# A decode step's forward and backward pass on one Trainium2 core: two zero fills at other places, and one late weight load through another queue

## The chip, the core and the metric

The kernel runs on one core of a Trainium2 chip. The core has a matrix engine (TensorE, PE in the profile), a vector engine (VectorE, DVE), an activation engine (ScalarE, ACT), GpSimd (POOL) and SyncE (SP), and 16 DMA engines that move data between the chip's memory (DRAM) and the core's on-chip memory. Two engines issue nearly all the transfers here: GpSimd, whose transfers stand in the profile as queue q0 (software_dynamic), and SyncE, queue q1 (hardware_dynamic). The metric is the device time of one execution in microseconds, as the median of several runs. Lower is better.

## What is computed

The reference is one token's pass through a transformer block with conditioning, and the gradients of all its inputs:

```python
mod = (silu(c) @ w_mod).reshape(c.shape[0], 6, 1, -1)   # sa, ca, ga, sb, cb, gb
h = layernorm(x) * (1 + ca) + sa
x = x + ga * attention(h, k_cache, v_cache, wq, wo)     # last 4096 of 65536 positions
h = layernorm(x) * (1 + cb) + sb
x = x + gb * glu(h, w_gate, w_up, w_down)               # sigmoid(h@w_gate) * (h@w_up) @ w_down
out, vjp = jax.vjp(f, x, k_cache, v_cache, wq, wo, w_gate, w_up, w_down, c, w_mod)
```

There are 11 outputs: the block's output and ten gradients. Two of them, the gradients of the two caches, have the caches' full size (4 heads by 65536 positions by 128), but attention reads the last 4096 positions only. So the first 61440 positions of each head are zeros, and the kernel has to write these zeros. They are 120 pieces of 1 MB, by far the largest part of what the kernel writes. The rest is the gradient of every weight matrix.

## The kernel before

**Stages.** The kernel first loads the first third of `w_mod`, the cache window, `A_wq` and the value window. It computes the modulation, the query and the scores of all 32 heads (the K pass), and the softmax. In the N passes (the loop over `g` and `t_`, 4 groups by 32 tiles, 128 steps; matmuls in line 737 into `n_ps`) it forms a matrix for each head from keys, values and probabilities. A long chain of matmuls with `A_wo` follows (`bch`, line 796, `b_ps`). Then come the feed-forward blocks `q` = 0 to 6 (`front`, `turn`), which load `w_up`, `w_gate` and `w_down` block by block, and last the weight gradients: outer products that DVE computes into a buffer of the arena, each sent to DRAM by one store of about 1 MB.

**The order is written out by hand.** The kernel is scheduled manually: each engine executes its instructions in the order of the source. GpSimd's queue in particular holds loads, zero fills and gradient stores in one fixed order, and an instruction that waits holds up everything behind it on that engine. Each issuing engine's DMAs also wait for the semaphore that they use; GpSimd's DMAs take eight semaphores in turn.

**Zero fills.** `zero(n, after)` takes the next `n` pieces from the list `zleft` and issues one DMA for each on GpSimd. If `after` is given, GpSimd waits for that instruction first. There are three kinds. A plain fill writes 1 MB from the tile `zeros` (line 209). In the N passes and in `bch`, pieces whose region is one row are copied from a piece of DRAM that is already zero (`big`, line 203). Six pieces, at fixed places in the list, are narrow: a tiny DMA (line 194) and 960 KB (line 197). How many pieces are taken at which place stands in constants at the top: `Z_SM` behind the softmax (line 595), `Z_N` over the 128 steps of the N passes (line 740; `spread(total, n)` deals `total` evenly over `n`), `Z_FFN` in the blocks, and `Z_HAND` behind the stores of the gradient of `w_down` near the end of the blocks.

**Stores of the gradient of `w_down`.** `dwd(q, off, outer)` computes four outer products into the 8 KB per partition at `off` and returns the store (line 1138). In block 5 stands `dwd(0)` with `zero(Z_HAND[0])` behind it, and at the end of the block `dwd(1)` with `zero(Z_HAND[1])`, `turn(6)`, and `dwd(2, 152)` with `zero(Z_HAND[2])`. Block 6 has `dwd(3)` with `zero(Z_HAND[3])`, and `dwd(4)` with `zero(Z_HAND[4])` follows. `dwd(5, 152)`, inside `layernorm_bwd_col`, uses the same place of the arena as `dwd(2, 152)`. The feed-forward's own loads of `w_down` go out on SyncE.

**The last stage.** `dw_rows(k, j, off)` writes one 128-row piece of the gradient of `w_up` or `w_gate` (store in line 1130), `sec(j)` one piece of the gradient of `w_mod`: it reduces the last sixth of `w_mod` against a row into `dcs` (the instruction of line 253), forms an outer product over the same buffer (line 249) and stores it (line 1260). For `j` < 6 that sixth is already on the chip. For `j` = 6 and 7 `sec_load(j)` fetches it, 256 KB each, into a part of `sec_t[j]`. `dwq_tile` (line 1308), `s2` (line 1312) and `kv_store` (line 1304) store the other gradients.

The order around `sec_load` in the source is: `dw_rows(1, 6)`, `dw_rows(1, 7)`, `sec(2)`, `sec(3)`, `sec_load(6)`, `sec_load(7)`, then the scores' gradient, and `grad_kv`, within which `sec(4)`, `dwq_tile(0)`, `sec(5)`, `dwq_tile(1)`, `sec(6)`, `dwq_tile(2)` stand at steps 8, 16 and 24.

Of the kernel before, what the change touches and what calls it, by code (L numbers as in the profile page):

```python
# [19 lines left out]
D = 1024  # L20
# [21 lines left out]
def spread(total, n):  # L42
    return [(i + 1) * total // n - i * total // n for i in range(n)]
# [6 lines left out]
Z_CB = 1  # L50
Z_Q = [0] * 6 + [1, 3]
Z_KC = [0] * 8
Z_SM = 5
Z_N = spread(34, 128)
Z_B = [n + (i in (31, 38)) for i, n in enumerate(spread(29, 43))] + [1, 1, 1, 1, 0] + [1, 0, 0, 1, 1, 1, 0, 0] + [1, 0, 1, 0, 1, 0, 0, 0]
Z_FOLD = (1, 1, 2, 3)
Z_FFN = [(1, 0, 1)] + [(1, 1, 1)] * 4 + [(0, 2)]
Z_HAND = (1, 1, 2, 1, 1)
Z_ROWS = (1, 1, 0, 0, 0, 0, 0, 0)
JT = 3  # L60
JV = KD - JT
# [1 line left out]
def kernel(  # L63
# [26 lines left out]
    nc = tc.nc  # L90
# [13 lines left out]
    def ar(off, size):  # L104
        return arena[:, int(off * KIB):int((off + size) * KIB)]
# [79 lines left out]
    def zero(n, after=None, big=False):  # L185
        for _ in range(n):
            if len(zleft) <= keep[0]:
                return
            region, narrow_ = zleft.pop(0)
            first = None  # L190
            if narrow_:
                nc.gpsimd.inc_swdge_sem([], [], mode="reset_dge_cursor")
                n = nlen - ncount.pop()
                first = nc.gpsimd.dma_start(
                    out=rest[0:NS, 0:nlen * 128].rearrange("p (t x) -> p t x", t=2)[:, :, n * 64:(n + 1) * 64],
                    in_=zeros[0:NS, 0:64].rearrange("p (t x) -> p t x", t=1).broadcast_to([NS, 2, 64]))
                ins = nc.gpsimd.dma_start(
                    out=region[8:P, :].bitcast(FP32).rearrange("(t p) x -> p t x", t=2),
                    in_=zeros[0:60, :].rearrange("p (t x) -> p t x", t=1).broadcast_to([60, 2, ZW // 2]))
            elif 119 - len(zleft) in UNEVEN:  # L200
                first = ins = uneven(region)
            elif big and region.shape[0] == 1:
                ins = nc.gpsimd.dma_start(  # L203
                    out=as_rows(region, BIGP).bitcast(FP32),
                    in_=zero_src[:, 0:P * ZW // 4].rearrange("i (p x) -> (i p) x", p=BIGP).bitcast(FP8))
            else:
                if region.shape[0] == 1:
                    region = as_rows(region, P)
                ins = nc.gpsimd.dma_start(out=region.bitcast(FP32), in_=zeros[:, :])  # L209
            if after is not None:  # L210
                dep(first or ins, after)
# [9 lines left out]
    def new_ps(name="ps"):  # L221
        p, tag = next_pool()
        return p.tile([P, 512], FP32, name=name, tag=tag)
# [131 lines left out]
    wm_view = w_mod.rearrange("(j p) n -> p j n", p=P)  # L355
# [238 lines left out]
    last = nc.vector.reciprocal(out=rsum, in_=ssum)  # L594
    zero(Z_SM, last)
    rs_ps = new_ps("rs_ps")[:, 0:P]
# [125 lines left out]
    def recent(mm, lag):  # L722
        last_mm.append(mm)
        return last_mm[-lag] if len(last_mm) >= lag else last_mm[0]

    for g in range(G):
        nbank = bank_pair("n_ps", g)
        for t_ in range(KT):
# [7 lines left out]
            for k in range(2):  # L736
                mm = nc.tensor.matmul(nbank[k][:, :], lhsT=k_nat[:, g, t_ * DH:(t_ + 1) * DH],  # L737
                                      rhs=vp[:, t_ % 2, 4 * k:4 * k + 4, :].rearrange("p h d -> p (h d)"),
                                      start=(t_ == 0), stop=False)
            zero(Z_N[s], recent(mm, 6), True)  # L740
            if t_ == 20:
# [375 lines left out]
    def dug_rows(k):  # L1117
        for q0 in range(0, NB, 2):
            n = min(2, NB - q0)
            tp = new_tp("tp_rows")  # L1120
            for b in range(4 * n):
                c0 = 8 * (q0 + b // 4) + 4 * k + b % 4
                nc.tensor.transpose(tp[:, b * P:(b + 1) * P], dug_all[:, c0:c0 + 1].broadcast_to([P, P]), ident_bf[:, :])
            nc.scalar.copy(out=dug_row[k][:, q0 * FB:(q0 + n) * FB].rearrange("p (s f j) -> p s f j", f=P, j=4),
                           in_=tp[:, 0:n * FB].rearrange("p (s j f) -> p s f j", f=P, j=4))

    def dw_rows(k, j, off, outer):
        t = ar(off, 7)
        outer(t, h2[:, j:j + 1], dug_row[k])
        nc.gpsimd.dma_start(out=(dwu_view, dwg_view)[k][:, j, :], in_=t)  # L1130

    def dwd(q, off, outer):
        t = ar(off, 8).rearrange("p (i d) -> p i d", i=4)
        for i in range(4):
            outer(t[:, i, :], hh_all[:, 4 * q + i:4 * q + i + 1], b1k)

        def store():
            nc.gpsimd.dma_start(out=wd_dram(out_8, q), in_=t)
        return store
# [7 lines left out]
    def turn(q, fills=0):  # L1147
        gates()
        turned(q, range(JT - 1))
        wd_ttr(0)  # L1150
        hh_ops(q)
        first = wd_ttr(1)
        ffn_mm(q, 0)
        if q + 1 < NB:
            load_wd(q + 1, 0, 2)
        ffn_mm(q, 2)
        turned(q, (JT - 1,))
        side(1)
        zero(fills, wd_ttr(2, 3))
        if q + 1 < NB:  # L1160
            load_wd(q + 1, 2, 2)
        last = dug_part(q)
        turned_mm(q)
        side(1)
        return first, last
# [6 lines left out]
    for q in range(NB):  # L1172
# [8 lines left out]
        for j in range(JT, KD):  # L1181
            w = ug_flat(q, j)
            ttr(w, w, dug_b, dh2acc[:, q * JV + j - JT:q * JV + j - JT + 1])
            if j == 3:
# [4 lines left out]
                elif more:  # L1189
                    zero(Z_FFN[q][1])  # L1190
                    dwd(0, 24, outer_dve)()
                    zero(Z_HAND[0])
                else:
                    dwd(3, 16, outer_dve)()
                    zero(Z_HAND[3])
        if q + 2 < NB:
# [4 lines left out]
        elif more:  # L1201
            dwd(1, 40, outer_dve)()
            zero(Z_HAND[1])
            turn(q + 1)
            dwd(2, 152, outer_dve)()
            zero(Z_HAND[2])
            dug_rows(0)
    dwd(4, 32, outer_dve)()
    zero(Z_HAND[4])
    dw_rows(0, 0, 40, outer_dve)  # L1210
# [35 lines left out]
    sec_t = [ar(o, 8) for o in (0, 8, 152, 16, 32, 40, 48, 56)]  # L1246
# [4 lines left out]
    late = [junk[:, i * P:(i + 1) * P] for i in range(8)]  # L1251

    def sec_load(j):
        nc.sync.dma_start(out=sec_t[j][:, 3 * D:4 * D], in_=wm_view[:, j, 5 * D:6 * D])

    def sec(j):
        w5 = g_t[j] if j < 6 else sec_t[j][:, 3 * D:4 * D]
# [58 lines left out]
    for b in range(2):  # L1316
        do4 = new_ps("do4")
        for i in range(KD):
            for a in range(4):
# [4 lines left out]
                       in_=do4.rearrange("q (a h r) -> q a h r", a=4, h=4))  # L1324
# [77 lines left out]
    sec(2)  # L1402
    sec(3)
    sec_load(6)
    sec_load(7)
    cp(dmod_bf[:, 0:8], dh1)
    mulv(dmod_bf[:, 8:16], dh1, ln1)
# [108 lines left out]
```

## Time and profile before

| | |
|---|---|
| median of 3 runs | 595.17 us (594.85 to 595.47) |
| the profiled execution: time | 596.39 us |
| the profiled execution: span, first to last instruction | 594.6 us |
| busy, share of the span | PE 72%, DVE 60%, ACT 42%, POOL 24% |
| data moved by the DMA engines | 246.58 MB |
| granted TensorE clock, mean | 0.802 |

The profile is of one execution. Its own time is 1.22 us above the median, and 1.8 us of it lie outside the span. In the views that follow, times are counted from the start of the span. A row of the windows gives for a stretch of time the busy time of each engine with its number of instructions, then the granted TensorE clock, the DMA share and the rate. The DMA share is the time of the packets that fall in the stretch, as a share of 16 engines; packets that overlap a little count twice, so a full stretch stands slightly above 1. A row of the timeline gives start, duration, engine, line, operation and tiles, and in brackets how long the engine was idle ahead of it and what ended that. A row of DMA issues ends with the median time from issue to landing.

### The profile page before, as it was taken

What the parts mean: (1) busy time and instruction counts of PE and PEld (TensorE: products, weight loads), DVE (VectorE), ACT (ScalarE), POOL (GpSimd) and SP (SyncE); (2) the same over time, 40 slices, a digit from 0 to 9 for tenths busy, and PEclk for the clock granted to TensorE, in tenths of its full rate; (3) what the DMA queues carried; (4) which work ended last, traced back from release to release, by engine and by line L of the source; (5) the groups of instructions that cost most, each with busy time, mean ns of one, the idle gap of its engine ahead of it and who ended that gap; (6) DMA issues with size and microseconds to landing.
All of it is one profiled execution on the core that took longest, in us unless ns stands there. A gap on an engine that the chain in (4) does not pass through costs nothing.

```text
span 594.6 us, 10189 instructions
## 1 busy us (share of the span) xinstructions
PE 429.0 (72%) x4167; PEld 247.9 (42%) x4196; DVE 354.8 (60%) x647; ACT 248.3 (42%) x398; POOL 143.5 (24%) x249
## 2 busy tenths in 40 slices
PE   3996778999999999997977667766676418275410
PEld 2784333322334545643544556655462408013100
DVE  3765479988931103029373866887987736596750
ACT  2489510545540103411224646665671436364410
POOL 3113113122122212122222312323122413123100
PEclk9999689999999999998998756777765655655555
DMA  8999999999999999999999999999999999999997
GB/s 351 422 418 421 423 464 392 425 425 428 424 409 458 419 438 429 414 404 451 413 408 399 418 409 408 400 411 409 424 382 428 423 429 421 425 408 413 409 413 321
DMA packets 32175, 246.58 MB, mean 415 GB/s; under 512 B 4781, under 2 KB 4781, under 8 KB 16816
## 3 DMA queue, kind: packets, MB, share of 16 engines
q0 software_dynamic: 26848, 225.98, 94.5%
q1 hardware_dynamic: 5232, 19.93, 9.3%
q8 instruction: 33, 0.54, 0.4%
q14 instruction: 14, 0.11, 0.1%
q10 hardware_dynamic: 48, 0.01, 0.0%
HBM read 79.17 MB, written 185.60 MB: 445 GB/s over the span
## 4 chain that ended last, share of the span: by engine, by line
PE 35%; DMA 30%; DVE 14%; issue 10%; ACT 5%; POOL 1%; ACTq 0%; POOLq 0%; DVEq 0%
DMA out_dram<-arena 13%; PE b_ps L796 12%; PE n_ps L737 9%; DMA out_dram<-out_dram 6%; DMA arena<-in_B_w_gate_dram 5%; PE t_ps L685 4%; DVE arena L253 3%; DMA out_dram<-zeros 3%; DMA arena<-in_B_w_up_dram 3%; DVE scr L253 2%; DVE arena L249 2%; ACT arena L524 2%; DVE arena L236 2%; PE tp_k L503 1%; PE w_ps L466 1%
## 5 line engine op out<-in xcount | busy, mean ns | idle before, releaser
L796 PE MATMUL b_ps<-arena 128*128 128x512 bf16 x493 | 116.2, 384 | 2.6 <-ACT arena L940 1.1
L236 DVE TENSOR_TENSOR arena<-arena 128x2048 bf16<-128x2048 bf16 x64 | 77.7, 1224 | 8.9 <-PE n_ps L737 5.3
L940 ACT COPY arena<-tp_side 128x1024 bf16<-128x1024 bf16 x62 | 61.0, 1015 | 51.5 <-PE tp_side L939 50.7
L796 PEld LDWEIGHTS <-arena 128*128 128x128 bf16 x512 | 49.0, 99 | 57.9 <-issue 5.1
L737 PE MATMUL n_ps<-arena 128*128 128x512 bf16 x246 | 66.3, 389 | 3.9 <-DVE arena L236 3.1
L203 POOL DMA_DIRECT2D out_dram<-out_dram x72 | 35.7, 497 | 127.5 <-PE n_ps L737 56.2
L939 PE MATMUL tp_side<-ident_bf,arena 128*128 128x128 bf16 x496 | 52.7, 278 | 8.8 <-DVE arena L236 5.4
L939 PEld LDWEIGHTS <-arena 128*128 128x128 bf16 x496 | 44.0, 128 | 17.7 <-issue 8.2
L693 ACT CAST arena<-t_ps 128x512 bf16<-128x512 f32 x56 | 28.9, 598 | 39.9 <-PE t_ps L685 39.9
L249 DVE TENSOR_SCALAR arena<-arena,h 128x3584 bf16<-128x3584 bf16 (+1 forms) x24 | 28.4, 1192 | 26.3 <-DMA out_dram<-arena 26.3
L1295 PE MATMUL ps_kv<-arena 32*128 32x512 bf16 x64 | 24.4, 588 | 26.1 <-DVE arena L257 16.1
L253 DVE CUSTOM_DVE_ANT_0 arena<-arena,scr 128x1024 bf16<-128x1024 bf16 x35 | 40.8, 1219 | 0.2
L1299 ACT ACTIVATE arena<-ps_kv 128x512 bf16<-128x512 f32 x48 | 25.4, 690 | 34.6 <-PE ps_kv L1295 34.4
L209 POOL DMA_DIRECT2D out_dram<-zeros x42 | 23.2, 555 | 58.3 <-DVE rows_all L236 24.9
L253 DVE CUSTOM_DVE_ANT_0 scr<-arena,b1k 128x1024 bf16<-128x1024 bf16 x28 | 34.2, 1222 | 4.0 <-DMA arena<-in_B_w_down_dram 3.6
L737 PEld LDWEIGHTS <-arena 128*128 128x128 bf16 x256 | 21.4, 99 | 35.7 <-issue 19.5
L245 DVE CAST arena<-b_ps 128x512 bf16<-128x512 f32 x6 | 4.1, 692 | 50.1 <-PE b_ps L796 50.1
L685 PE MATMUL t_ps<-arena 128*32 128x512 bf16 x256 | 24.1, 399 | 3.4 <-ACT arena L760 2.8
L1295 PEld LDWEIGHTS <-arena 32*128 32x128 bf16 x64 | 6.9, 116 | 42.4 <-issue 41.6
L524 ACT COPY arena<-tp_wq 128x1024 bf16<-128x1024 bf16 x23 | 21.4, 1067 | 7.3 <-PE tp_wq L522 7.3
L1077 ACT COPY arena<-tp_ug 128x1024 bf16<-128x1024 bf16 x21 | 20.5, 1008 | 7.7 <-PE tp_ug L1076 7.7
L965 POOL DMA_DIRECT2D arena<-in_B_w_up_dram x14 | 10.7, 767 | 40.7 <-DVE dh2acc L253 26.6
(325 smaller groups left out, 665.6 us busy)
## 6 DMA issues: line engine op xcount, KB each, us to landing
out_dram<-zeros POOLq DMA_DIRECT2D x42, 1024.0 KB, 12.1
out_dram<-arena POOLq DMA_DIRECT2D x35, 1024.0 KB, 12.4
out_dram<-arena POOLq DMA_DIRECT2D x16, 896.0 KB, 13.5
arena<-in_A_wq_dram POOLq DMA_DIRECT2D x8, 1024.0 KB, 20.9
arena<-in_A_wo_dram POOLq DMA_DIRECT2D x8, 1024.0 KB, 13.4
arena<-in_w_mod_dram POOLq DMA_DIRECT2D x7, 1024.0 KB, 18.9
arena<-in_B_w_up_dram POOLq DMA_DIRECT2D x14, 512.0 KB, 10.1
arena<-in_B_w_gate_dram POOLq DMA_DIRECT2D x14, 512.0 KB, 14.6
```

Source lines behind the costliest of these rows:

```text
L203: ins = nc.gpsimd.dma_start(out=as_rows(region, BIGP).bitcast(FP32), in_=zero_src[:, 0:P * ZW // 4].rearrange("i (p x) -> (i p) x", p=BIGP ...
L236: return nc.vector.tensor_tensor(out=out, in0=a, in1=b, op=op)
L249: return nc.vector.tensor_scalar(out=out, in0=a, scalar1=s1, scalar2=None, op0=op0)
L253: return nc.vector.tensor_tensor_reduce(out=out, in0=w, in1=b, scale=1.0, scalar=0.0, op0=ALU.mult, op1=ALU.add, accum_out=acc)
L524: nc.scalar.copy(out=blk, in_=tp[:, :])
L685: nc.tensor.matmul(ps[32 * hh:32 * hh + 32, :].rearrange("p (j m) -> p j m", j=4), lhsT=N_sb[:, h * P + a:(h + 1) * P - 3 + a:4], rhs=a4[: ...
L693: nc.scalar.copy(out=o, in_=v)
L737: mm = nc.tensor.matmul(nbank[k][:, :], lhsT=k_nat[:, g, t_ * DH:(t_ + 1) * DH], rhs=vp[:, t_ % 2, 4 * k:4 * k + 4, :].rearrange("p h d -> ...
L796: mm = nc.tensor.matmul(bbank[p][k][:, :], lhsT=a4[:, p, h, :], rhs=wo_t[u][:, a, k * 512:(k + 1) * 512], start=(i == 0 and a == 0), stop= ...
L939: nc.tensor.transpose(tp[:, i * P:(i + 1) * P], blk[:, i * P:(i + 1) * P], ident_bf[:, :])
L940: nc.scalar.copy(out=blk if dst is None else dst, in_=tp[:, :])
L1295: nc.tensor.matmul(ps[:, :], lhsT=rows[r, t8 * P:(t8 + 1) * P], rhs=bd[r, :], start=True, stop=True, tile_position=(32 * tc_, 0))
```

## The change

```diff
-Z_SM = 5
-Z_N = spread(34, 128)
+Z_SM = 6
+Z_N = spread(33, 128)
...
-Z_HAND = (1, 1, 2, 1, 1)
+Z_HAND = (1, 2, 1, 1, 1)
...
     def sec_load(j):
-        nc.sync.dma_start(out=sec_t[j][:, 3 * D:4 * D], in_=wm_view[:, j, 5 * D:6 * D])
+        nc.gpsimd.dma_start(out=sec_t[j][:, 3 * D:4 * D], in_=wm_view[:, j, 5 * D:6 * D])
```

Three edits. The softmax is followed by six fills in place of five, and 33 in place of 34 are dealt over the N passes; the pieces are the same pieces in the same order, so the first one that the N passes took is now taken behind the softmax, and each later one stands about one place earlier, less and less so towards the end of the passes. Behind `dwd(1)` two pieces are taken in place of one, and behind `dwd(2)` one in place of two: one plain fill passes from behind `dwd(2)`'s store to ahead of it. The two late loads of `w_mod` leave SyncE's queue and stand in GpSimd's, behind the store of `sec(3)` and ahead of that of `sec(4)`. On PE, DVE and ACT the order of instructions stays the same, the kinds of fills and their numbers too, and the number of bytes.

## The prediction

> **What bounds the kernel now.** I read the page's slices and its table of DMA queues first, then the windows, then the timelines of GpSimd, SyncE and DVE around the three edits.
>
> ```profile
> PE 429.0 (72%) x4167; PEld 247.9 (42%) x4196; DVE 354.8 (60%) x647; ACT 248.3 (42%) x398; POOL 143.5 (24%) x249
> DMA  8999999999999999999999999999999999999997
> q0 software_dynamic: 26848, 225.98, 94.5%
> q8 instruction: 33, 0.54, 0.4%
> ```
>
> The second row is the mean busy share of the 16 DMA engines in 40 slices; of the other two, one is the queue with nearly all the traffic, the other fetches instructions. The DMA engines are full from the second slice to the last but one, while PE is busy for 72% of the span and DVE for 60%. So the bytes set the time: the change moves none of them away, and can gain only where DMA engines now stand still or work badly. The windows show where that is.
>
> ```profile
> 10.00:434.00 424.00, 357.61 (x3464) 204.01 (x3494) 252.32 (x434) 181.22 (x296) 102.23 (x179) 0.89 1.06 420
> 434.00:434.50 0.50, 0.50 (x6) 0.46 (x5) 0.50 (x2) 0.50 (x1) 0.00 (x0) 0.50 0.79 295
> 434.50:435.00 0.50, 0.36 (x5) 0.23 (x3) 0.50 (x2) 0.50 (x2) 0.00 (x0) 0.50 0.62 246
> 435.00:435.50 0.50, 0.50 (x8) 0.50 (x6) 0.50 (x2) 0.50 (x1) 0.07 (x1) 0.50 0.61 229
> 435.50:436.00 0.50, 0.50 (x7) 0.39 (x6) 0.50 (x1) 0.36 (x2) 0.50 (x2) 0.50 0.62 229
> 436.00:436.50 0.50, 0.50 (x7) 0.50 (x6) 0.50 (x3) 0.50 (x1) 0.50 (x2) 0.50 0.40 147
> 436.50:437.00 0.50, 0.36 (x5) 0.20 (x3) 0.50 (x2) 0.50 (x2) 0.50 (x2) 0.50 1.13 459
> 436.50:590.00 153.50, 67.65 (x682) 40.66 (x679) 97.34 (x195) 61.70 (x97) 35.74 (x56) 0.56 1.03 419
> 590.00:592.90 2.90, 0.00 (x0) 0.00 (x0) 0.00 (x0) 0.00 (x0) 0.00 (x0) 0.50 0.38 161
> ```
>
> The last two figures of a row are the DMA share and the rate. There is one gap, from 434.0 to 436.5 us: shares of 0.79, 0.62, 0.61, 0.62 and 0.40 lack (0.21 + 0.38 + 0.39 + 0.38 + 0.60) × 0.5 = 0.98 us of all 16 engines. Two things matter in it. The share falls in steps: some engines have nothing left already between 434.0 and 434.5, but 0.40 × 16, about six, still work at 436.5. The end of the kernel looks the same: from 590.0 to 592.9 the share is 0.38, so engines finish one after another over nearly 3 us. So each engine works through its own part of the transfers, and the time is that of the last engine. The third place is a dip rather than a gap:
>
> ```profile
> 520.00:522.00 2.00, 0.00 (x0) 0.00 (x0) 2.00 (x4) 0.00 (x0) 0.51 (x1) 0.50 1.02 427
> 522.00:523.00 1.00, 0.00 (x0) 0.00 (x0) 1.00 (x3) 0.00 (x0) 0.02 (x1) 0.50 1.01 414
> 523.00:524.00 1.00, 0.00 (x0) 0.00 (x0) 0.93 (x7) 0.00 (x0) 0.43 (x1) 0.50 0.92 349
> 524.00:525.00 1.00, 0.37 (x1) 0.10 (x1) 1.00 (x2) 0.00 (x0) 0.11 (x1) 0.50 1.08 423
> 525.00:526.00 1.00, 0.92 (x5) 0.27 (x4) 1.00 (x2) 0.69 (x2) 0.00 (x0) 0.50 1.00 352
> 526.00:527.00 1.00, 1.00 (x5) 0.30 (x3) 1.00 (x3) 1.00 (x3) 0.00 (x0) 0.50 0.96 354
> 527.00:528.00 1.00, 1.00 (x4) 0.49 (x4) 1.00 (x2) 1.00 (x3) 0.13 (x1) 0.50 1.06 424
> ```
>
> From 522 to 528 the rate is 414, 349, 423, 352, 354 and 424 GB/s, where the row ahead has 427. Against the 424 of the last one that lacks (10 + 75 + 1 + 72 + 70) / 424 = 0.54 us. These are the microseconds in which SyncE's loads of `w_mod` run beside GpSimd's stores.
>
> **The change part by part.** The sum is made against the profiled execution, 596.39 us; the median of the runs is 1.22 us lower, and I take the same difference off it.
>
> *Fill from the N passes to behind the softmax.*
>
> ```profile
> 66.35 2.65 POOL L209 DMA_DIRECT2D out_dram<-zeros  x5 [8.14 <-DVE rsum L594]
> 74.96 0.53 POOL L209 DMA_DIRECT2D out_dram<-zeros  x1 [5.95 <-PE n_ps L737]
> 66.00:94.00 28.00, 23.46 (x164) 10.63 (x163) 20.27 (x36) 6.18 (x26) 5.68 (x11) 0.82 1.13 447
> 84.00:104.00 20.00, 18.01 (x83) 6.48 (x82) 18.55 (x18) 1.09 (x2) 5.90 (x11) 0.94 1.05 416
> 90.00:102.00 12.00, 10.51 (x55) 3.89 (x56) 11.81 (x13) 1.09 (x2) 4.44 (x8) 1.00 0.94 358
> ```
>
> The fill that is issued at 74.96 goes out right behind the five at 66.35 to 69.00, in one issue of 0.53 us while GpSimd is idle. It is the same kind of fill. The DMA share from 66 to 94 us is 1.13, so an earlier issue starts nothing earlier; it lengthens the list by one transfer, and each fill of the passes then stands about one place ahead. The loads of `A_wo` stand behind them, one more piece (1.05 MB / 427 GB/s = 2.5 us) late at first; their readers, the chain of line 796, begin 70 us later. The only thin place is 90 to 102: share 0.94, 0.06 × 12 = 0.7 us if all of it were standstill. Around it, over 20 us, the share is 1.05, as in the whole first part (1.06). Bounds 0 and −0.7; I take 0, by the 20 us row.
>
> *Fill ahead of `dwd(2)`'s store.*
>
> ```profile
> 426.61 0.66 POOL L197 DMA_DIRECT2D out_dram<-zeros  x1
> 435.44 0.57 POOL L1138 DMA_DIRECT2D out_dram<-arena  x1 [8.16 <-DVE arena L249]
> 436.00 1.08 POOL L209 DMA_DIRECT2D out_dram<-zeros  x2
> 446.01 1.67 DVE L249 TENSOR_SCALAR arena<-b1k,hh_all 128x1024 bf16<-128x1024 bf16 x4
> out_dram<-arena POOLq DMA_DIRECT2D x1, 1024.0 KB, 5.3
> ```
>
> GpSimd is idle for 8.16 us ahead of 435.44, until DVE has the product. The added issue at 427.3 falls into that. Its 2.5 us of DMA work reach from 434.3 to 436.8 on the engines that run dry first, so the gap closes. Behind it `dwd(2)` lands up to 2.5 us later than its 435.44 + 5.3 = 440.7; its place is written again by `dwd(5)` at 446.01, 2.8 us after that. What does the closed gap bring? If all engines kept their lead to the end, 0.98 us. But the engines that finish last at 436.5 stood still for next to nothing, and later issues wait for whole landings, those of the last engine:
>
> ```profile
> 505.74 1.16 DVE L249 TENSOR_SCALAR arena<-arena,h 128x3584 bf16<-128x3584 bf16 x1 [4.64 <-DMA out_dram<-arena]
> 517.44 1.16 DVE L249 TENSOR_SCALAR arena<-arena,h 128x3584 bf16<-128x3584 bf16 x1 [3.53 <-DMA out_dram<-arena]
> 532.22 1.22 DVE L253 CUSTOM_DVE_ANT_0 arena<-arena 128x1024 bf16<-128x1024 bf16 x1
> ```
>
> DVE stands at 505.74 and 517.44 until a store has landed whole. A lead of the early engines is given back there. So bounds 0 and −0.98; I take −0.2, near the last engines' end, since the row 436.0 to 436.5 still has six at work.
>
> *The late load through GpSimd.*
>
> ```profile
> 522.11 1.03 SPq L1254 DMA_DIRECT2D arena<-in_w_mod_dram  x2
> 523.57 0.53 POOL L1260 DMA_DIRECT2D out_dram<-arena  x1 [1.55 <-DVE dh_hl L245]
> 527.87 1.02 POOL L1260 DMA_DIRECT2D out_dram<-arena  x1 [3.76 <-DVE arena L249]
> out_dram<-arena POOLq DMA_DIRECT2D x5, 1024.0 KB, 8.6
> arena<-in_w_mod_dram SPq DMA_DIRECT2D x2, 256.0 KB, 10.3
> ```
>
> SyncE now issues both at 522.11, and they land 10.3 us later. On GpSimd they follow `sec(3)`'s store: two issues of 0.53 to 1.02 us from 524.1, inside the 3.76 us in which GpSimd waits for `sec(4)`; nothing behind them is delayed. `sec(3)`'s store lands about 523.57 + 8.6 = 532.2, and with the 0.5 MB no longer beside it (1.25 us) near 531; the loads follow 0.6 and 1.2 us later, 531.6 and 532.2. `sec(6)` reads the first at 532.22, `sec(7)` the second some 8 us after that. So DVE waits for nothing, or a few tenths. On the DMA engines the bytes stay; what may go is the dip. Stores and loads mixed in GpSimd's queue ran at 420 GB/s over the first 434 us, so I take −0.4 of the 0.54; bounds 0 and −0.54.
>
> The Trainium skill (DMA: Bandwidth & Descriptors, Rules for kernel authors) says that spreading transfers over SP, ACT and GpSimd brings no bandwidth, as they share the same 16 engines. By that rule the move back brings none either; this term would be 0 and the sum −0.2. The dip to 349 GB/s speaks against it, without saying what causes it.
>
> Sum: 0 − 0.2 − 0.4 = −0.6 us: 595.8 for the profiled execution, 594.6 for the median.
>
> **The rivals.** *All engines gain.* If the order in which engines run late is not kept from 436 to 592, the gap counts in full: −0.98 − 0.54, and some 0.1 from the thin place, −1.6: 593.6. For it speaks that the gap is real and the fill covers it; against it the six engines at 436.5.
>
> *Nothing happens.* The last engine neither stood still nor shared: 595.2. For it: shares of 1.06 and 1.03 on both sides of the gap.
>
> *Slower: the load comes late, and the DMA list runs out behind it.* DVE would wait at 532.22 for the load, and with it `sec(6)`'s store, behind which GpSimd holds all others.
>
> ```profile
> 535.06 1.02 POOL L1260 DMA_DIRECT2D out_dram<-arena  x1 [1.93 <-DVE arena L249]
> arena<-in_w_mod_dram POOLq DMA_DIRECT2D x7, 1024.0 KB, 18.9
> ```
>
> What is issued by 533 lasts about 8.6 us, to 541. A store issued at 435.44 reaches the engines by 436.5, so 535.06 may slip by some 4.5 us; from a landing at 536.7 on, each further microsecond costs one. GpSimd's loads of `w_mod` took 18.9 us elsewhere, which would be 543.0, and 6 us lost; half way between that and the threshold it is 3 us: 598.2. Against it: only some 8.6 us of work stand in the list here.
>
> The Trainium skill (SBUF — State Buffer, SBUF: two separate sides) states that GpSimd cannot write a transfer's descriptors while DVE holds their shared port, and gives 3.1 us in place of 0.62; two loads would start some 5 us late by that, an estimate, and DVE is busy here without a break. The rows have 1.02 in place of 0.53, so I see at most a small part of it.
>
> *Slower: the last engine gets more.* The order of transfers decides which engine is busy when instructions are fetched (q8: 33 packets, 0.4% of 16 × 594.6 us, 1.15 us each). One more of them on the last engine: 595.2 + 1.2 = 596.4.
>
> **How the numbers follow.** Forecast 0.40, all engines 0.30, nothing 0.12, late load 0.10, last engine 0.08. A change within 0.2% (1.2 us) can hardly be told from none here. Faster: 0.30 and a small part of the forecast's case, 0.32; within: 0.50; slower: 0.18. The forecast's own range is 594.0 to 595.2. The range for 8 in 10 takes in all three terms at their far ends (−0.98 − 0.54, and half of the 0.7 of the thin place: 593.3) and most of the last engine's case (596.1).
>
> **What would show it.** The windows from 434 to 436.5 have a share near 1, and the tail beyond 590 gets flatter rather than ending much sooner: then engines lead, but the last does not. If the end moves by 1 us or more with a tail as steep as now, the first rival holds. The rate between 522 and 532 stays above 400; DVE at `sec(6)` shows a wait under 1 us. A wait of 4 us there, followed by a DMA share under 1 near 541, would be the slower case.

## The result and the profile after

| | median (lowest to highest) | against before, 95% interval |
|---|---|---|
| before | 595.53 us (594.85 to 596.17, 8 runs) | |
| after | 593.95 us (593.31 to 594.63, 8 runs) | 0.9972 (0.9961 to 0.9983) |
| after, measured again with the experiments | 594.42 us (593.20 to 595.18, 11 runs; before 595.76) | 0.9979 (0.9970 to 0.9988) |

The change saves 1.3 to 1.6 us; the forecast was 0.6. The profiled execution of after took 593.89 us, near its median; that of before, 596.39 us, stands 0.9 us above the median of these runs, so clock times in the two traces differ by more than the change is worth. The page of after, engines, slices of DMA share and the main queue:

```profile
PE 427.6 (72%) x4196; PEld 245.0 (41%) x4196; DVE 354.8 (60%) x647; ACT 248.1 (42%) x398; POOL 143.8 (24%) x251
DMA  9999999999999999999999999999999999999997
q0 software_dynamic: 27008, 226.51, 94.9%
```

DMA still sets the time and the bytes are the same. The places of the second and third edit, in GpSimd's timeline of after (start, duration, line, and in brackets the idle time ahead):

```profile
425.80 0.57 POOL L209 DMA_DIRECT2D out_dram<-zeros  x1
434.26 0.56 POOL L1138 DMA_DIRECT2D out_dram<-arena  x1 [7.89 <-DVE arena L249]
434.81 0.53 POOL L209 DMA_DIRECT2D out_dram<-zeros  x1
...
521.34 1.09 POOL L1254 DMA_DIRECT2D arena<-in_w_mod_dram  x2
525.11 1.02 POOL L1260 DMA_DIRECT2D out_dram<-arena  x1 [2.69 <-DVE arena L249]
```

One fill now goes out at 425.80, ahead of the 7.89 us in which GpSimd waits for DVE's product. The two loads are two issues of 1.09 us together, and GpSimd then still waits 2.69 us for `sec(4)`. The windows of after (last two figures: DMA share, GB/s):

```profile
434.00:434.50 0.50, 0.19 (x4) 0.07 (x2) 0.50 (x1) 0.50 (x2) 0.24 (x1) 1.00 1.07 410
434.50:435.00 0.50, 0.46 (x8) 0.45 (x8) 0.50 (x1) 0.50 (x1) 0.50 (x2) 1.00 1.14 426
435.00:435.50 0.50, 0.19 (x4) 0.07 (x2) 0.50 (x3) 0.50 (x2) 0.34 (x1) 1.00 1.13 426
435.50:436.00 0.50, 0.34 (x4) 0.22 (x4) 0.50 (x3) 0.50 (x1) 0.00 (x0) 1.00 1.03 377
436.00:436.50 0.50, 0.12 (x3) 0.12 (x3) 0.50 (x2) 0.50 (x2) 0.00 (x0) 1.00 1.23 475
436.50:587.50 151.00, 65.12 (x675) 38.62 (x673) 96.14 (x192) 60.15 (x95) 35.52 (x56) 0.57 1.02 419
587.50:590.40 2.90, 0.00 (x0) 0.00 (x0) 0.00 (x0) 0.00 (x0) 0.00 (x0) 0.50 0.48 201
...
516.00:520.00 4.00, 0.00 (x0) 0.00 (x0) 4.00 (x6) 0.00 (x0) 1.07 (x2) 0.50 0.95 395
522.00:528.00 6.00, 5.92 (x17) 1.69 (x16) 6.00 (x8) 5.46 (x12) 1.99 (x3) 0.50 1.00 379
525.00:526.00 1.00, 1.00 (x5) 0.35 (x3) 1.00 (x2) 1.00 (x3) 0.89 (x1) 0.50 0.85 295
```

The gap of before is gone: every half microsecond from 434.0 to 436.5 has a share above 1. (The granted TensorE clock in these rows is 1.00, before 0.50. That is not what counts: sm_hand and narrow7 below have 0.50 from 434 to 436.5 and gain as much.) The rate over the rest is the 419 GB/s of before. The last 2.9 us ahead of the same distance from the span's end have a share of 0.48, before 0.38, so 0.52 × 2.9 = 1.5 us lack there in place of 1.8: the tail didn't get flatter, the end moved. The dip at the loads is still there, 379 GB/s from 522 to 528 with 295 in its worst microsecond, and a new thin place stands at 516 to 520 (0.95). For these two stretches, before:

```profile
516.00:520.00 4.00, 0.00 (x0) 0.00 (x0) 2.56 (x4) 0.00 (x0) 0.53 (x1) 0.50 1.02 430
522.00:528.00 6.00, 3.29 (x10) 1.17 (x11) 5.93 (x14) 2.69 (x6) 0.69 (x3) 0.50 1.00 386
```

### The profile page after: what moved, and what is told of

Same layout as the page of the kernel before. It is cut to its first block, busy times and chain, and to the rows that moved or that the text cites. A ratio compares the mean times of both kernels' runs of the same rounds, so it can differ in the third digit from the quotient of the medians.

```text
span 592.1 us, 10214 instructions
## 1 busy us (share of the span) xinstructions
PE 427.6 (72%) x4196; PEld 245.0 (41%) x4196; DVE 354.8 (60%) x647; ACT 248.1 (42%) x398; POOL 143.8 (24%) x251
## 4 chain that ended last, share of the span: by engine, by line
PE 32%; DMA 31%; DVE 16%; issue 9%; ACT 5%; POOL 2%; ACTq 0%; POOLq 0%; DVEq 0%
DMA out_dram<-arena 11%; PE b_ps L796 9%; PE n_ps L737 9%; DMA out_dram<-out_dram 7%; DMA arena<-in_B_w_gate_dram 5%; DVE arena L253 4%; PE t_ps L685 4%; DMA arena<-in_w_mod_dram 3%; DVE arena L249 3%; DVE scr L253 3%; DMA out_dram<-zeros 3%; ACT arena L524 2%; DMA arena<-in_B_w_down_dram 2%; DVE arena L236 2%; PE tp_k L503 1%
## 5 line engine op out<-in xcount | busy, mean ns | idle before, releaser
L796 PE MATMUL b_ps<-arena 128*128 128x512 bf16 x512 | 118.6, 384 | 1.1 <-ACT arena L940 1.1
L796 PEld LDWEIGHTS <-arena 128*128 128x128 bf16 x512 | 48.9, 99 | 58.1 <-issue 5.4
L737 PE MATMUL n_ps<-arena 128*128 128x512 bf16 x256 | 67.7, 389 | 3.4 <-DVE arena L236 2.9
L939 PE MATMUL tp_side<-ident_bf,arena 128*128 128x128 bf16 x496 | 50.3, 269 | 9.8 <-DVE arena L236 5.5
L939 PEld LDWEIGHTS <-arena 128*128 128x128 bf16 x496 | 41.7, 123 | 18.5 <-issue 9.1
L1295 PE MATMUL ps_kv<-arena 32*128 32x512 bf16 x64 | 24.4, 588 | 24.6 <-DVE arena L257 14.3
L737 PEld LDWEIGHTS <-arena 128*128 128x128 bf16 x256 | 21.4, 99 | 35.6 <-issue 19.4
L1053 PE MATMUL fg<-arena,h_bf 128*32 128x256 bf16 x224 | 15.0, 404 | 8.1 <-DMA arena<-in_B_w_gate_dram 8.0
```

Of the source, the lines that this page charges most:

```text
L796: mm = nc.tensor.matmul(bbank[p][k][:, :], lhsT=a4[:, p, h, :], rhs=wo_t[u][:, a, k * 512:(k + 1) * 512], start=(i == 0 and a == 0), stop= ...
L939: nc.tensor.transpose(tp[:, i * P:(i + 1) * P], blk[:, i * P:(i + 1) * P], ident_bf[:, :])
L1295: nc.tensor.matmul(ps[:, :], lhsT=rows[r, t8 * P:(t8 + 1) * P], rhs=bd[r, :], start=True, stop=True, tile_position=(32 * tc_, 0))
```

## The experiments

Theory A is the forecast's reason (early engines lead through the gap, and the lead is given back where DVE waits for whole landings), theory B the first rival (the gap counts in full). Each ratio is against before on the same chip in the same minutes; kernels that weren't measured side by side are compared by their ratios.

**The three edits, each alone.**

```diff
# sm_only
-Z_SM = 5
-Z_N = spread(34, 128)
+Z_SM = 6
+Z_N = spread(33, 128)
# hand_only
-Z_HAND = (1, 1, 2, 1, 1)
+Z_HAND = (1, 2, 1, 1, 1)
# load_only
-        nc.sync.dma_start(out=sec_t[j][:, 3 * D:4 * D], in_=wm_view[:, j, 5 * D:6 * D])
+        nc.gpsimd.dma_start(out=sec_t[j][:, 3 * D:4 * D], in_=wm_view[:, j, 5 * D:6 * D])
```

> Only the fill that moves from the N passes to behind the softmax. By my forecast (the last DMA engine sets the end, and no engine stands still there) the time stays at that of before: ratio 1.000, within 0.3 us. By the rival that every gap counts in full it gains about 0.1 us. By what the two traces now show (whole landings are 0.45 us earlier from 156 us on, and 0.7 us at 430) it gains 0.5 to 0.7 us: ratio 0.9990, and the thin place of 96 to 98 us is gone from the windows.

> Only the fill that moves ahead of the store of dwd(2). By the forecast it gains 0.2 us (0.9997), since the engines that finish last had stood still for next to nothing; by the rival that the gap counts in full, 1.0 us (0.9983). Either way the windows from 434 to 436.5 have a DMA share of 1.

> Only the late load of w_mod through GpSimd. By the forecast it gains 0.4 us (0.9993) by taking the dip of 522 to 528 us away; by the rule that the queue makes no difference 0; by the traces of before and after, where stores that follow the loads lost some 0.3 us of their lead, it loses up to 0.3 us (1.0005). The rate between 522 and 528 tells it: above 410 GB/s by the forecast, some 390 by the others.

Measured: sm_only 595.51 us, 0.9998 (0.9989 to 1.0007); hand_only 594.43 us, 0.9984 (0.9975 to 0.9993); load_only 595.81 us, 1.0004 (0.9995 to 1.0013). Only the fill ahead of `dwd(2)` is worth something: 0.0016 × 595.5 = 0.95 us (0.4 to 1.5 by the interval), with a gap of 0.98 us. That is theory B's price, and the forecast's 0.2 us lies outside. load_only's rate from 522 to 528 is 401 GB/s, between the two values expected, but the dip is still there. It stands later, as the loads do (issued at 523.6 in place of 522.1):

```profile
527.00:528.00 1.00, 1.00 (x5) 0.40 (x4) 1.00 (x2) 1.00 (x4) 0.61 (x1) 0.50 1.07 360
528.00:529.00 1.00, 1.00 (x4) 0.20 (x2) 1.00 (x2) 1.00 (x3) 0.82 (x2) 0.50 0.82 299
```

Theory A says where the gain should have vanished, and sm_only, whose time is that of before and whose profiled execution took just its median, is the right trace to hold it against. DVE's two long waits for a whole landing, timeline of sm_only:

```profile
504.86 1.15 DVE L249 TENSOR_SCALAR arena<-arena,h 128x3584 bf16<-128x3584 bf16 x1 [4.57 <-DMA out_dram<-arena]
516.55 1.15 DVE L249 TENSOR_SCALAR arena<-arena,h 128x3584 bf16<-128x3584 bf16 x1 [3.53 <-DMA out_dram<-arena]
```

The same of hand_only:

```profile
503.57 1.15 DVE L249 TENSOR_SCALAR arena<-arena,h 128x3584 bf16<-128x3584 bf16 x1 [3.36 <-DMA out_dram<-arena]
515.01 1.15 DVE L249 TENSOR_SCALAR arena<-arena,h 128x3584 bf16<-128x3584 bf16 x1 [3.53 <-DMA out_dram<-arena]
```

Both still wait for a landing, but the landing comes 1.29 and 1.54 us earlier; 0.23 us of that was there already when `dwd(2)`'s store started (434.56 and 434.33). The spans differ by 593.7 − 592.7 = 1.0 us. So the lead is not given back at these waits. The time from the start of a store's DMA to its landing, for the stores of line 1130 issued from 488 to 498 us, first before:

```profile
DMA to landing us min/median/max: 12.8/15.0/17.0
```

and hand_only:

```profile
DMA to landing us min/median/max: 11.6/13.5/15.3
```

By then the landings themselves are 1.5 us shorter (sm_only: 15.0; after: 13.5).

**Two edits together.** sm_hand has both fills and leaves the load on SyncE; hand_load has the fill ahead of `dwd(2)` and the load through GpSimd, without the softmax edit.

> The two fills without the load: the whole change but for the load. If the load brings nothing, it has the time of the changed kernel, ratio 0.9972 to before; if the load gains 0.4 us, 0.9979; if it loses 0.3 us, 0.9967. If the two fills gain only what the forecast gives them (0.2 us), 0.9997.

> The change without its softmax edit: the fill ahead of dwd(2) and the load through GpSimd. If each edit counted by itself (softmax 0, fill 1.0 us, load -0.3 us), this kernel has the time of the changed one, ratio 0.9972. If a lead from the softmax edit is thrown away in the gap at 434 us and counts once the gap is closed, this kernel is 0.6 to 0.9 us slower than the changed one: 0.9985 to 0.9988. And against the fill alone (0.9984) it shows the price of the load once more: equal, or up to 0.3 us slower.

Measured: sm_hand 593.56 us, 0.9969 (0.9958 to 0.9980); hand_load 594.99 us, 0.9986 (0.9977 to 0.9995). With sm_hand at 0.9969 against hand_only's 0.9984, and after at 0.9972 against hand_load's 0.9986, it looked as if the softmax edit, worth nothing alone, were worth 0.15% once the gap is closed. The intervals overlap in both pairs; further runs below did not bear it out.

**The gap made wider.** The fill is taken from behind `dwd(1)` instead, so that nothing stands ahead of `dwd(2)`'s store. (The piece due there is a narrow one with its two DMAs; it goes out behind the store.)

```diff
-Z_HAND = (1, 1, 2, 1, 1)
+Z_HAND = (1, 0, 3, 1, 1)
```

> The opposite edit: Z_HAND is (1, 0, 3, 1, 1), so the narrow fill of 960 KB passes from ahead of the store of dwd(2) to behind it, and the list runs out 2.3 us earlier, at about 432. If a gap counts in full, the time rises by what the gap grows, 2.0 to 2.4 us: ratio 1.0034 to 1.0040. If the DMA engines made up for a part of it later, or only the engines that finish last counted (these now stand still for nearly all of the added 2.3 us as well), at least 1.8 us. Under 1 us would speak for a bound other than the DMA engines.

Measured: 598.16 us, 1.0039 (1.0026 to 1.0053), so 0.0039 × 595.6 = 2.3 us lost. The window around the gap, before:

```profile
430.00:438.00 8.00, 6.21 (x70) 5.50 (x71) 6.25 (x15) 5.46 (x7) 1.65 (x3) 0.50 0.93 358
```

and gap_wide:

```profile
430.00:438.00 8.00, 6.82 (x76) 6.11 (x77) 6.25 (x16) 5.22 (x7) 3.10 (x5) 0.50 0.61 246
```

(0.93 − 0.61) × 8 = 2.56 us of all 16 engines more are lost in the gap, and the end moves by 2.3 (1.5 to 3.2 by the interval). By the medians the gap counts in full in this direction too. The profiled execution was the fastest of its four, 597.19 us; in it the stretch from the start of `dwd(2)`'s store to the end is 1.4 to 1.8 us longer than in before, sm_only and load_only, which have the gap of before.

**The new thin place filled.** sm_hand, and the fill that is issued at about 459 us goes instead between the stores of `dw_rows(1, 6)` and `dw_rows(1, 7)`:

```diff
-Z_ROWS = (1, 1, 0, 0, 0, 0, 0, 0)
+Z_ROWS = (1, 0, 0, 0, 0, 0, 0, 1)
```

> The two fills of the change without the load, and one more fill moved: Z_ROWS is (1, 0, 0, 0, 0, 0, 0, 1), so the fill behind the second store of dw_rows (at 459 us) stands between the stores of dw_rows(1, 6) and dw_rows(1, 7), at 512. In the kernels with the gap closed the rate falls to 337 to 394 GB/s at 516 to 518 us, before the load. If that is standstill, it gains 0.2 to 0.4 us on the two fills alone (0.9969 to 0.9964) and the rate at 516 to 518 is above 415. If the last engines have work there anyway, it is the same as the two fills.

Measured: 593.35 us, 0.9962 (0.9949 to 0.9974). Its windows:

```profile
516.00:520.00 4.00, 0.41 (x1) 0.10 (x1) 3.93 (x10) 0.00 (x0) 1.06 (x2) 0.50 1.09 429
522.00:528.00 6.00, 6.00 (x16) 1.54 (x15) 6.00 (x7) 6.00 (x13) 3.00 (x4) 0.50 1.01 420
```

The thin place has 429 GB/s, after 395. And the dip from 522 to 528 is gone, 420 for 379, although the loads of `w_mod` go out on SyncE here as before. So the dip was not made by the loads' queue: it goes when 1 MB more stands in the list ahead of them (they land 12.4 us after their start here, 9.7 us in sm_hand).

**A seventh narrow piece.** sm_hand, and one more plain fill is written as a narrow piece.

```diff
-NARROW = (15, 45, 75, 93, 103, 113)
+NARROW = (15, 45, 75, 93, 103, 113, 118)
```

> The two fills of the change without the load, and a seventh narrow piece in place of a plain one, at place 118 of the list (at 450 us). A narrow piece gives some of the 16 engines one packet less (120 packets in place of 128). If the time is that of the last engine and this engine is among the ones relieved, the end comes up to 0.3 us sooner (0.9964) and the tail beyond 588 us gets steeper; if it is not, the time is that of the two fills (0.9969) or up to 0.3 us longer.

Measured: 594.05 us, 0.9969 (0.9956 to 0.9981), as sm_hand. It tells nothing apart.

**Softmax edit and load, with no thin place left.** thin_nosm is thin_fill without the softmax edit (`Z_SM = 5`, `spread(34, 128)`); thin_load is thin_fill with the load through GpSimd.

> thin_fill without the softmax edit (Z_SM = 5, spread(34, 128)): the gap at 434 to 436.5 us is closed and the thin place at 516 to 520 is filled. If the softmax edit is worth 0.15% where the gap is closed, as the two pairs so far say (sm_hand 0.9969 against hand_only 0.9984, the change 0.9972 against hand_load 0.9986), this stands near 0.9977 (594.2 us), against 0.9962 with the edit, and its stretch from 90 to 102 us is thin (DMA share near 0.95). If the two pairs were chance and the edit is worth nothing, as it was alone (sm_only 0.9998), it stands at 0.9962, 593.3 us.

> thin_fill with the two loads of w_mod through GpSimd as well. If the load through GpSimd is worth nothing, as in the three pairs so far (load_only 1.0004; hand_load 0.56 us above hand_only; the change 0.39 us above sm_hand, each within its uncertainty), this stands at 0.9962 to 0.9969, 593.3 to 593.7 us. If the loads gain by closing the dip behind 522 us where nothing else is thin there, it stands at 0.9953 or below, 592.8 us. A small loss of 0.3 to 0.5 us would be a fourth pair on that side.

Measured: thin_nosm 593.29 us, 0.9959 (0.9946 to 0.9971); thin_load 592.87 us, 0.9952 (0.9939 to 0.9966). Without the softmax edit the time is the same, so what the pairs above hinted at fell. The load through GpSimd is at most a small gain here, within the uncertainty. thin_load also shows what a late load costs, in DVE's timeline at `sec(6)`:

```profile
529.58 1.23 DVE L253 CUSTOM_DVE_ANT_0 arena<-arena 128x1024 bf16<-128x1024 bf16 x1 [2.02 <-DMA arena<-in_w_mod_dram]
```

DVE waits 2.02 us for it, and this is the kernel with the lowest time of all. Its DMA rate stays between 419 and 428 GB/s in each stretch of five microseconds from 525 to 545, so the DMA list didn't run out behind the wait.

**The fill alone and the whole change, again, side by side.**

> The fill ahead of the store of dwd(2) alone, measured a second time, beside the whole change in the same call. In the first measurements it stood at 0.9984 (594.43 us) and the change at 0.9972 (593.95 us). If the softmax edit and the load add 0.5 us or more to it, it stands at least 0.5 us above the change again, near 0.9984. If they add nothing, as thin_nosm (0.9959 without the softmax edit, 0.9962 with it) says of the one, both stand within 0.3 us of each other, at 0.9972 to 0.9980, and the fill alone is the change.

> The change itself, measured a second time beside the fill alone. 0.9972 (593.95 us) in the first measurement. If the softmax edit and the load add something to the fill, it stands at least 0.5 us below the fill alone; if not, within 0.3 us of it.

Measured: the fill alone 594.20 us, 0.9976 (0.9967 to 0.9985); the change 594.42 us, 0.9979 (0.9970 to 0.9988). They are equal within the uncertainty, about 0.5 us: as far as these runs tell, the fill ahead of `dwd(2)` is the whole gain.

**Beyond both.** thin_load (0.9952, up to 0.9966) is faster than before, and than the change as measured the second time (0.9979, from 0.9970); the interval of the change's first measurement (0.9961 to 0.9983) overlaps with it. The three kernels with the thin place filled stand at 0.9952 to 0.9962 (mean 0.9958), the seven results with the gap closed and the thin place open at 0.9969 to 0.9986 (mean 0.9976), so that filling is worth about 0.18%, 1.1 us. The rate says as much: sm_hand moves 406 GB/s from 515 to 535, thin_fill 424, which is 20 × 18 / 424 = 0.85 us. So does the stretch from the start of `dwd(2)`'s store to the end of the span: 157.0 to 157.2 us in the three, 157.8 us in the mean of the seven.

## Why the prediction came out as it did

**The bound.** Right: DMA sets the time, and the change's only gain came from where engines stood still.

**Fill behind the softmax, 0.** Right by sm_only (0.9998), thin_nosm beside thin_fill, and hand_again beside change_again. In sm_only's windows the thin place of the N passes is full:

```profile
90.00:102.00 12.00, 10.63 (x56) 3.96 (x56) 11.81 (x12) 1.08 (x2) 4.42 (x8) 1.00 1.04 415
430.00:438.00 8.00, 7.09 (x79) 6.38 (x80) 6.24 (x15) 5.02 (x6) 2.11 (x4) 0.50 0.92 353
```

Share 1.04 there, before 0.94. But the place is not always thin without the edit. hand_only, which lacks the edit:

```profile
90.00:102.00 12.00, 10.79 (x63) 3.84 (x61) 11.63 (x12) 1.09 (x2) 4.42 (x8) 1.00 1.06 426
```

The seven kernels with the edit have 1.04 to 1.07 there, the seven without it 0.94 to 1.06. No lead shows further on either: `dwd(2)`'s store starts at 434.1 to 435.0 us with the edit and at 434.2 to 435.4 without it. And if a lead of 0.7 us were lost in the gap, whose end DVE's product sets, it would lower the share of the eight microseconds by 0.09; sm_only has 0.92, before 0.93. Where the bytes moved sooner from 90 to 102 are lost again stays open.

**Fill ahead of `dwd(2)`, −0.2 of at most −0.98.** This is the step that failed. The gap closes as worked out; the value taken was not what it is worth. It rested on "the engines that finish last at 436.5 stood still for next to nothing" and "a lead of the early engines is given back there", at DVE's two long waits. Measured: −0.95 us (hand_only) and 0.0024 × 595.8 = −1.4 us (hand_again), so the gap in full. gap_wide bears it out with 2.3 us for 2.56. At the two waits the landings come 1.29 and 1.54 us earlier in hand_only than in sm_only.

The stretch from the start of `dwd(2)`'s store to the end of the span, which leaves out what differed earlier in an execution, gives the price once more, from one execution of each kernel: 158.8 to 159.2 us, in the mean 159.0, in before, sm_only and load_only, which have the gap, and 156.9 to 158.4, in the mean 157.8, in the seven results with the gap closed and the thin place open. That is 1.2 us, so the bound of 0.98 was a little low. It was counted against a share of 1, where the stretch ahead of the gap has 1.06. By the rates, the five rows have 229 GB/s in the mean, and (420 − 229) / 420 × 2.5 = 1.1 us lack.

If each DMA engine works through a list of its own, as the prediction has it, the engines that finish last in the gap are not those that set the landings 70 us later; the condition that the first rival named, that the order of late engines isn't kept, fits. That it is another engine which is last by then is argued, not shown: the traces don't tell the DMA engines apart, and no run tests whether each has its own list.

**Late load through GpSimd, −0.4 of at most −0.54.** Mis-sized: it measured 0, to about 0.5 us. load_only stands at 1.0004 (from 0.9995, where the forecast was 0.9993); hand_load beside hand_only, after beside sm_hand and thin_load beside thin_fill differ by +0.02%, +0.03% and −0.10%, all within the uncertainty. The reason given, that the dip comes from loads on SyncE beside GpSimd's stores, falls with two rows: after keeps the dip (379 GB/s) with the load on GpSimd, thin_fill loses it (420) with the load on SyncE. From 522 to 532 the rate of after is 398 GB/s, before 400; the sign named for a gain was a rate above 400. The rule of the Trainium skill that was weighed against this term (DMA: Bandwidth & Descriptors, Rules for kernel authors: spreading transfers over the issuing engines brings no bandwidth) agrees with these runs: 1.0004 alone. The rest of this step was right. The wait of "nothing, or a few tenths" at `sec(6)`, in DVE's timeline of after:

```profile
503.25 1.15 DVE L249 TENSOR_SCALAR arena<-arena,h 128x3584 bf16<-128x3584 bf16 x1 [3.16 <-DMA out_dram<-arena]
514.68 1.15 DVE L249 TENSOR_SCALAR arena<-arena,h 128x3584 bf16<-128x3584 bf16 x1 [3.55 <-DMA out_dram<-arena]
529.73 1.23 DVE L253 CUSTOM_DVE_ANT_0 arena<-arena 128x1024 bf16<-128x1024 bf16 x1 [0.18 <-DMA arena<-in_w_mod_dram]
```

**The sum.** −0.6 against −1.3 to −1.6: the fill's term was 0.8 to 1.2 us too small, the load's 0.4 too large. The first rival's −1.6 is nearer to both measurements. For the gap the runs bear it out, that it counts in full; its 0.54 for the dip they don't. That the measured time lies within the range for 8 in 10 (593.3 to 596.1) is owed to its lower end, which counts the gap and the dip in full as the rival does, and not to the mechanism of the forecast. That two wrong terms, one too small and one too large, partly make up for each other is luck.

**The other rivals.** Nothing happens: out, by the intervals. The late load: the wait is 0.18 us, and thin_load's 2.02 us cost nothing, as that rival's slack of some 4.5 us would have it; the starts some 5 us late that were estimated by the Trainium skill (SBUF — State Buffer, SBUF: two separate sides), for a DVE that holds the shared port, did not occur. The two issues took 1.09 us in all beside a busy DVE; whether DVE held the port then, no trace here tells. The last engine gets more: nothing points to it.

## What to carry to other kernels

Where the DMA engines set the time, add up what lacks in a gap, against the share and rate of the full stretches beside it, and count it in full, as it counted here, even if some engines work through it; don't argue it away from which engines look last at that moment. A row of low rate at a transfer is not yet the work of its queue: see whether the list ahead of it is thin, and put bytes there. And an effect of 0.15% is not shown by pairs whose intervals overlap: two such pairs agreed on one that further runs did not bear out.

## What the runs showed of the hardware

Two things were not expected. The time from a store's start to its landing is no measure of what a gap costs: for the stores of line 1130 from 488 to 498 us its median is 15.0 us in before and 13.5 in hand_only, but 14.1 in gap_wide, the slowest kernel, and 14.3 in thin_load, the fastest. And a stretch can have a DMA share of 1.00 at 386 or 379 GB/s (522 to 528) where 1.01 stands beside 420 in thin_fill: a full share is not a full rate, and the two columns have to be read together.
